# Where a chunk's key transposes and state products stand on TensorE, and a planner that counts a change of weight shape

## The chip, the cores and the metric

One core of a Trainium2 chip runs the whole kernel. The metric is the device time of one execution in microseconds (us), the median of the runs shown: 847.98 us of three runs (847.36 to 849.97). The profile is one further execution.

## The reference, cut to what matters

The kernel computes three stages in a row:

- A gated linear attention over 4 batches, 8 heads, 768 steps and head size 48: `state = f * state + k v^T`, `y = q state`, with `f` the sigmoid of `f_logit`.
- A two-layer network on the 3072 tokens (384 to 2048 to 384) with a leaky activation `max(h,0) + alpha*min(h,0)`.
- A routed layer of 8 experts (384 to 1024 to 384, ReLU). Tokens are dealt out by sorted gate logits with room for 384 tokens per expert; each token goes to one expert.

```python
for t in range(S):
    state = f[:, :, t, :, None] * state + np.einsum('bhd,bhe->bhde', k[:, :, t], v[:, :, t])
    y[:, :, t] = np.einsum('bhd,bhde->bhe', q[:, :, t], state)
...
g = np.maximum(h, 0.0) + alpha * np.minimum(h, 0.0)
...
out[mask] = np.maximum(x[mask] @ w1[e], 0.0) @ w2[e]
```

## The kernel before, in words

**The work.** Attention runs in 24 chunks of 128 steps (6 a batch, chunk i is number i % 6 of its batch). Three chunks make a block of 384 rows, eight blocks in all; a block's rows then go through the network (`ffn1`, line 1061) in products of 384 or 392 columns, here called FFN products. The attention of block b+1 is recorded with a lower number of priority than the FFN of block b (10b+10 against 10b+11), so on each engine it goes first wherever both could start. Beside blocks 0 and 1 the weights of the network are converted and split on VectorE and ScalarE (`narrow`, `split`); later the experts' weights are.

**A chunk** (`chunk`, line 1009) has these steps on TensorE; each fp32 product is two instructions in the trace, a transpose one:

- `s2` (line 900), on VectorE: the decayed keys `kT`, then the decayed queries `qT`.
- `s3` (909), the scores: 8 products, weights of 64 rows by 128 columns, into two PSUM banks; 16 instructions. Then two VectorE products with the causal mask write `A`, one for each bank; they are kept as `a["done"]`.
- `s3k` (924), the keys transposed: 4 transposes with weights of 128 by 128 into one bank, which ScalarE copies to `kt`. The last chunk of a batch has none.
- `s4` (935), the rows: weights of 128 by 64, 12 products with `A` and `v`, and 8 with the old state where the chunk isn't the first of its batch; 24 or 40 instructions of 128 columns. They are recorded `behind(a["done"])`.
- `s4s` (966), the state's products: 8 products of `kt` (128 by 64) and `v`, 16 instructions of 48 columns. Two VectorE operations on 64 partitions then make the new state, which the rows of the next chunk need. The last chunk of a batch has none.
- `s5` (988): ScalarE and VectorE turn the rows into the rounded input of the network.

The steps share three PSUM banks (`bank`, line 659, `bufs=3`): scores take two, transposes, rows and state's products one each.

**The order.** Nothing of this runs in the order in which it is written. `Plan.record` (206) keeps every operation with a price (`cost`, 544), and `Plan.schedule` (328) deals them out on a made-up clock: again and again it takes, over all engines, the operation that could start first; among those of one time the lowest priority number, then the one recorded first. VectorE may pass over one for another up to `PATIENCE` = 170 ns later. `behind(ops)` (182) makes a *soft* dependence: the operation is offered only once all of `ops` have been given a start. It is no semaphore; it only changes the order. The order so found is what every engine's queue then holds, and on the chip an instruction waits for its own inputs and for all that stands ahead of it in its queue.

Where the planner sees TensorE idle it puts filler products (`fill`, 448; line 1670 in the profile) of 512 columns into a free bank; nothing reads them. TensorE's price is the product's columns at 2.4 GHz (twice that at the slow clock), with nothing for what stood ahead of it:

```python
            price = op.cost[e]
            if e == "tensor":
                self.fill(free[e], t)
                slow = self.slow(t)
                if op.load:
                    mm[1] = max(mm) + op.load * slow
                    t = max(t, mm[1])
                price *= slow
```

An fp32 product with one side of 64 costs `2 * max(m, n) / 1.2 / 2 + 4`, so 110.7 ns for a score or a row product and 57.3 ns for one of the state's; a transpose costs 110 ns.

Of the kernel before, what the change touches and what calls it, by code (L numbers as in the profile page):

```python
# [28 lines left out]
HP = H // 2  # L29
# [48 lines left out]
SAME = {"vector": 125.0, "scalar": 150.0}  # L78
PATIENCE = 170.0
URGENT = 80.0  # L80
WINDOW, BUSY = 10240 / 3, 3060.0

LAGS = {"tensor": 200.0, "vector": 165.0, "scalar": 150.0, "gpsimd": 110.0, "sync": 120.0}
# [51 lines left out]
class Op:  # L135
    def __init__(self, idx, engines, calls, prio):
        self.idx, self.engines, self.calls, self.prio = idx, engines, calls, prio
        self.deps, self.soft, self.next, self.first, self.uses = set(), set(), [], [], []
        self.cost, self.load, self.columns, self.bytes, self.held = {}, 0.0, 0.0, 0, ()
        self.extra = 0.0  # L140

    def arenas(self):
        return {g.tag.arena for g in self.uses if g.tag.arena}
# [2 lines left out]
class Plan:  # L146
# [59 lines left out]
    def record(self, engines, method, a, k, slack=0.0):  # L206
        outs = accesses(a[:1]) + accesses(k.get(n) for n in ("out", "accum_out"))
        ins = accesses(a[1:]) + accesses(x for n, x in k.items() if n not in ("out", "accum_out"))
        if method == "matmul" and not (k["start"] and k["stop"]):

            outs = [self.ghosts[outs[0].tensor.name].ap]
        op = self.add(engines, lambda e, b: getattr(e, method)(*[b(x) for x in a], **{n: b(x) for n, x in k.items()}), outs, ins)  # L212
        op.slack = slack
        for e in engines:
            op.cost[e] = cost(e, method, outs, ins)
        if method in ("matmul", "transpose") and ins[0].dtype in (F32R, BF):
            op.load = free_size(ins[0]) / 1.2 if ins[0].dtype == F32R else 27.0
            op.held = {o for o, b in self.written.get(ins[0].tensor.name, []) if o is not op and meets(region(ins[0]), b)}
        if "tensor" in engines:
            n = free_size(ins[1]) if method == "matmul" else 256  # L220
            rows = ins[0].ap[0][1] / 128 * (0.5 if free_size(ins[0]) == 64 else 1.0)
            op.columns = n * rows * (4 if method == "matmul" and ins[0].dtype == F32 else 1)
        if "dma" in method:
            op.bytes = dma_bytes(outs + ins)
            op.extra = self.extra if "indirect" in method else 0.0
        return op
# [101 lines left out]
    def schedule(self):  # L328
# [10 lines left out]
        free["tensor"] = 800.0  # L339
        avail = {e: [] for e in self.ENGINES}  # L340
        mm, hw, dma = [0.0, 0.0], 600.0, [0.0, 0.0]

        def offer(op):
            since = max([g.since for g in op.uses if g.slot] + [d.start for d in op.soft], default=0.0)
# [21 lines left out]
        for _ in ops:  # L366
            best = None
            for e in self.ENGINES:
                wait, own, near = PATIENCE if e == "vector" else 0.0, None, []
                for op in avail[e]:  # L370
                    since = max(op.ready[e], free[e])
                    if best is not None and since > best[0] or own is not None and since > own[0] + wait:
                        continue
                    t = first(op, e)
                    if t is None or len(op.engines) > 1 and not self.better(op, e, t, free):
                        continue
                    key = (t, op.prio, op.idx, e, op)
                    if wait:
                        near.append(key)
                    if own is None or key < own:  # L380
                        own = key
                if near:

                    h = min((k for k in near if k[0] <= own[0] + wait), key=lambda k: k[1])
                    if URGENT <= h[1] < own[1] and own[0] + own[4].cost[e] > h[0] + 60.0:
                        fits = [k for k in near if k[0] + k[4].cost[e] <= h[0] + 60.0]
                        own = min(fits, default=h)
                if own is not None and (best is None or own < best):
                    best = own
            assert best, "no instruction can start"  # L390
            t, _, _, e, op = best
            for x in op.engines:
                avail[x].remove(op)
            for g in op.first:
                g.since, g.slot = self.place(g, ())
                g.slot.busy = True
                g.tag.given += 1
            price = op.cost[e]
            if e == "tensor":
                self.fill(free[e], t)  # L400
                slow = self.slow(t)
                if op.load:
                    mm[1] = max(mm) + op.load * slow
                    t = max(t, mm[1])
                price *= slow
                mm[0] = t
                self.count(t, t + price, op.columns)
            op.engine, op.start = e, t
            for a in op.arenas():
                a.left, a.turn = a.left - 1, max(a.turn, t + 1.0)  # L410
            free[e] = op.end = t + price
            if op.bytes:
                at = op.end
                if e == "sync":
                    hw = at = max(hw, at) + 450.0
                lane = e == "sync"
                dma[lane] = max(dma[lane], at + 650.0) + op.bytes / (300.0 if lane else 200.0)
                op.end = dma[lane] + 1000.0 + op.extra
            for g in op.uses:
                g.uses -= 1  # L420
                g.end = max(g.end, op.end)
                if not g.uses:
                    g.slot.busy, g.slot.free = False, g.end + 100.0
            for n in op.next:
                n.left -= 1
                if not n.left:
                    offer(n)
# [206 lines left out]
class Kernel:  # L634
# [265 lines left out]
    def s2(self, i):  # L900
        nc, a = self.nc, self.A[i]
        n = HP * SEG
        for name, dec in (("k", a["qr"][:, 1:n + 1].rearrange("p (g t) -> p g t", g=HP)[:, :, 1:]),
                          ("q", a["pf"].rearrange("p (g t) -> p g t", g=HP)[:, :, 1:])):
            t = a[name + "T"] = self.ap.tile([128, HP, C], F32, name=name + "T", bufs=2)
            self.claim(t)
            nc.vector.tensor_tensor(t, a[name], dec, OP.mult)

    def s3(self, i):

# [13 lines left out]
    def s3k(self, i):  # L924
# [3 lines left out]
        p = self.bank()  # L928
        t = a["kt"] = self.ap.tile([128, HP, 128], F32, name="kt", bufs=2)
        self.claim(t)  # L930
        for g in range(HP):
            nc.tensor.transpose(p[:, g * 128:(g + 1) * 128], a["kT"][:, g, :], self.ident)
        nc.scalar.activation(t.rearrange("p a b -> p (a b)"), p, AF.Copy)

    def s4(self, i):
# [30 lines left out]
    def s4s(self, i):  # L966
# [2 lines left out]
        if c == NCH - 1:  # L969
            return  # L970
        p = self.bank()
        for g in range(HP):
            for s in range(2):
                r = slice(s * 64, s * 64 + 64)
                nc.tensor.matmul(p[r, g * D:(g + 1) * D], a["kt"][:, g, r], a["v"][:, 2 * g + s, :D], start=True, stop=True)
        pv = p[:, :HP * D].rearrange("p (g e) -> p g e", g=HP)
        new = self.st[(i + 1) % 2]
# [874 lines left out]
```

## Time and profile before

| what | number |
|---|---|
| median of three runs | 847.98 us (847.36 to 849.97) |
| profiled execution | 851.19 us |
| its span, first to last instruction | 849.3 us |
| around the span | 1.89 us |
| TensorE busy | 820.0 us, 97% |
| VectorE busy | 564.8 us, 66% |
| ScalarE busy | 349.6 us, 41% |
| mean granted TensorE clock | 0.989 |

PE is TensorE's products, PEld its weight loads, DVE VectorE, ACT ScalarE, POOL GpSimd. A timeline row merges instructions of one kind that follow each other; its second number runs to the modelled end of the last, which reaches into the next row, so what a group takes of TensorE is read from its start to the start of the next row. Rows, state's products, and their joint runs all show as `bank<-early 128*64`: x40 is a chunk's rows, x16 of 48 columns its state's products, x56 the two together; `64*128` is the scores, and x32 that begins with them is scores and state's products together. FFN products carry `rounded` and `weights`.

### The profile page before, as it was taken

The numbers are of one execution on the slowest core, as the hardware profiler recorded it, in microseconds if no ns is written. First come the engines' busy times: TensorE is split into PE (matmuls) and PEld (weight loads), VectorE is DVE, ScalarE is ACT, GpSimd is POOL, SyncE is SP. The second block draws the span as 40 slices with busy tenths as digits, with TensorE's granted clock in tenths as the row PEclk, the third lists the DMA queues.
The fourth block names the chain that finished last, engine by engine and source line by source line (L and its number), as shares of the span: only waits on it lengthen the run. The fifth ranks groups of instructions, "written<-read, shape, count | busy, mean of one in ns | idle before, by whom it ended". The sixth has DMA issues, their size and how long they took to land. (4 is left out here: it accounts for less than half of the span.)

```text
span 849.3 us, 16038 instructions
## 1 busy us (share of the span) xinstructions
PE 820.0 (97%) x6122; PEld 756.5 (89%) x6122; DVE 564.8 (66%) x1308; ACT 349.6 (41%) x742; POOL 113.9 (13%) x105
## 2 busy tenths in 40 slices
PE   6999989999999999999999999999999999999995
PEld 3687889999999999999999999888788999899995
DVE  6899976977866966966975754655767658452220
ACT  3577665355555355555455443420122212222220
POOL 3111011210200200300300000000202302311211
PEclk7999999999999999999999999999999999999998
DMA  8895202599889688988878770003878775687400
GB/s 177 221 315 135 48 20 75 136 289 281 231 274 292 136 291 256 236 278 279 248 237 290 251 240 29 1 10 134 312 277 329 316 288 183 246 314 230 164 28 33
DMA packets 92792, 172.60 MB, mean 203 GB/s; under 512 B 31674, under 2 KB 61378, under 8 KB 92706
## 3 DMA queue, kind: packets, MB, share of 16 engines
q1 hardware_dynamic: 89490, 162.04, 60.0%
q0 software_dynamic: 3072, 9.44, 3.2%
q8 instruction: 50, 0.82, 0.4%
q14 instruction: 36, 0.29, 0.1%
q10 hardware_dynamic: 144, 0.01, 0.0%
HBM read 111.69 MB, written 59.77 MB: 202 GB/s over the span
## 5 line engine op out<-in xcount | busy, mean ns | idle before, releaser
L212 PE MATMUL bank<-rounded,weights 128*128 128x384 f32 (+1 forms) x1740 | 354.4, 344 | 1.2 <-POOL weights L212 0.5
L212 PE MATMUL bank<-weights,rounded 128*128 128x392 f32 (+1 forms) x1620 | 325.1, 344 | 3.0 <-ACT weights L212 2.3
L212 PEld LDWEIGHTS bank<-rounded,weights 128*128 128x128 f32 (+1 forms) x1740 | 302.4, 187 | 7.7 <-issue 2.3
L212 PEld LDWEIGHTS bank<-weights,rounded 128*128 128x128 f32 x1620 | 287.5, 189 | 5.6 <-issue 3.2
L212 ACT ACTIVATE rounded<-bank 128x384 fp32r<-128x384 f32 x110 | 54.1, 492 | 201.1 <-PE bank L212 188.4
L212 DVE TENSOR_TENSOR early<-early 128x384 fp32r<-128x384 f32 (+2 forms) x196 | 120.0, 629 | 16.1 <-ACT early L212 15.1
L212 PEld LDWEIGHTS bank<-early 128*64 128x64 f32 (+2 forms) x1696 | 98.3, 153 | 20.9 <-issue 10.4
L212 PE MATMUL bank<-early 128*64 128x128 f32 (+3 forms) x1696 | 110.2, 269 | 2.7 <-DVE early L212 1.5
L212 DVE SCALAR_TENSOR_TENSOR common<-common,rest,bank 128x384 f32<-128x384 f32 x128 | 77.9, 608 | 47.1 <-ACT common L232 46.1
L212 ACT ACTIVATE early<-early 128x384 fp32r<-128x384 f32 (+2 forms) x177 | 95.4, 548 | 31.9 <-DMA wd<-early 20.4
L212 POOL TENSOR_TENSOR rounded<-common,rounded 128x384 fp32r<-128x384 f32 x36 | 49.4, 1373 | 435.0 <-ACT rounded L212 398.0
L232 ACT ACTIVATE common<-bank 128x384 f32<-128x384 f32 x128 | 62.6, 489 | 71.4 <-PE bank L212 70.9
L212 ACT ACTIVATE rounded<-common 128x384 fp32r<-128x384 f32 x118 | 62.0, 525 | 65.9 <-DVE common L212 62.8
L212 DVE SCALAR_TENSOR_TENSOR rounded<-bank,rounded 128x384 fp32r<-128x384 f32 x62 | 34.5, 556 | 50.2 <-ACT rounded L212 48.3
L212 DVE TENSOR_TENSOR rounded<-common,rounded 128x384 fp32r<-128x384 f32 x82 | 46.5, 566 | 28.7 <-ACT rounded L212 20.3
L212 DVE TENSOR_TENSOR_SCAN early<-early 128x516 f32<-128x516 f32 x48 | 61.9, 1289 | 1.9 <-ACT early L212 1.6
L212 ACT ACTIVATE common<-bank 128x384 f32<-128x384 f32 x48 | 23.3, 492 | 71.4 <-PE bank L212 69.7
L212 POOL DMA_INDIRECT out_dram<-common,late x24 | 25.5, 1061 | 167.8 <-ACT common L212 115.7
L212 DVE TENSOR_TENSOR late<-late,cols 128x1536 bf16<-128x1536 bf16 (+3 forms) x53 | 42.7, 817 | 0.2
L212 POOL DMA_INDIRECT common<-x2d,late x24 | 25.9, 1077 | 90.2 <-DVE late L212 58.6
L212 DVE TENSOR_TENSOR rounded<-bank,rounded 128x384 fp32r<-128x384 f32 x48 | 26.3, 555 | 10.8 <-ACT rounded L212 10.3
L212 DVE TENSOR_TENSOR early<-bank,mask 128x512 f32<-128x512 f32 x48 | 31.0, 684 | 3.2 <-PE bank L212 2.9
(110 smaller groups left out, 488.7 us busy)
## 6 DMA issues: line engine op xcount, KB each, us to landing
wd<-early SPq DMA_DIRECT2D x128, 384.0 KB
weights<-wd SPq DMA_DIRECT2D x64, 768.0 KB
early<-in_w_dram SPq DMA_DIRECT2D x64, 384.0 KB
early<-in_fkq_dram SPq DMA_DIRECT2D x46, 288.0 KB
raw<-in_w_in_dram SPq DMA_DIRECT2D x16, 384.0 KB
raw<-in_w_out_dram SPq DMA_DIRECT2D x16, 384.0 KB
early<-in_v_dram SPq DMA_DIRECT2D x24, 192.0 KB
x2d<-common SPq DMA_DIRECT2D x24, 192.0 KB
```

The lines of the kernel that those rows point to most:

```text
L212: op = self.add(engines, lambda e, b: getattr(e, method)(*[b(x) for x in a], **{n: b(x) for n, x in k.items()}), outs, ins)
L232: return e.activation(b(out), b(x), AF.Relu, scale=-1.0)
```

## The change

The planner keeps the form of the last TensorE operation: how many rows its weights have, and whether they have 64 columns. Where an operation's form differs from the last one's, its start is put off by 92 ns; where the form is the same but the last was short (price up to 130 ns) and this one isn't, by 72 ns; and after either, the next operation by 80 ns. This is added to the made-up clock after the choice of the operation; fillers don't change the form. `s2` keeps its two products as `a["rows"]`; the transposes of `s3k` stand behind them; the products of `s4s` stand behind `a["done"]`, the masks of the chunk's scores, as the rows do.

```diff
+TURN, LONGER, AGAIN = 92.0, 72.0, 80.0
...
+            op.form = ins[0].ap[0][1], free_size(ins[0]) == 64
...
+        form, short, again = None, False, 0.0
...
                 slow = self.slow(t)
+                t, again = t + again, 0.0
+                turn = TURN if op.form != form else LONGER if short and price > 130.0 else 0.0
+                if turn:
+                    t, again = t + turn, AGAIN
+                form, short = op.form, price <= 130.0
                 if op.load:
...
             nc.vector.tensor_tensor(t, a[name], dec, OP.mult)
+        a["rows"] = self.last(2)
...
-        for g in range(HP):
-            nc.tensor.transpose(p[:, g * 128:(g + 1) * 128], a["kT"][:, g, :], self.ident)
+        with self.behind(a["rows"]):
+            for g in range(HP):
+                nc.tensor.transpose(p[:, g * 128:(g + 1) * 128], a["kT"][:, g, :], self.ident)
...
-        for g in range(HP):
-            for s in range(2):
-                r = slice(s * 64, s * 64 + 64)
+        for g, s in [(g, s) for g in range(HP) for s in range(2)]:
+            r = slice(s * 64, s * 64 + 64)
+            with self.behind(a["done"]):
                 nc.tensor.matmul(p[r, g * D:(g + 1) * D], a["kt"][:, g, r], a["v"][:, 2 * g + s, :D], start=True, stop=True)
```

## Rows read from the trace of the kernel before

**Rows 1.** The page: busy time of the engines, granted clock in 40 slices.

```profile
PE 820.0 (97%) x6122; PEld 756.5 (89%) x6122; DVE 564.8 (66%) x1308; ACT 349.6 (41%) x742; POOL 113.9 (13%) x105
...
PEclk7999999999999999999999999999999999999998
```

**Rows 2.** Windows, all instructions: PE, PEld, DVE, ACT, POOL busy; clock, DMA.

```profile
0.00:41.76 41.76, 33.76 (x273) 20.12 (x274) 31.69 (x71) 16.78 (x33) 10.08 (x19) 0.88 0.84 196
41.76:123.40 81.64, 75.38 (x576) 68.08 (x575) 77.47 (x151) 58.70 (x142) 13.04 (x11) 1.00 0.51 138
...
163.60:560.00 396.40, 395.20 (x2897) 378.08 (x2894) 280.81 (x525) 199.43 (x412) 34.39 (x23) 1.00 0.72 224
560.00:620.00 60.00, 57.12 (x459) 47.74 (x458) 36.80 (x143) 5.91 (x12) 6.46 (x6) 1.00 0.50 190
```

**Rows 3.** Windows, the fillers (line 1670) alone: PE busy, PEld busy, clock, DMA.

```profile
0.00:41.76 41.76, 17.28 (x52) 5.53 (x52) 0.88 0.84 196
41.76:123.40 81.64, 4.26 (x16) 1.57 (x16) 1.00 0.51 138
...
560.00:620.00 60.00, 7.43 (x29) 2.47 (x29) 1.00 0.50 190
```

**Rows 4.** PE's timeline, chunks 7 and 8: start us, us, instruction, count.

```profile
149.99 1.76 PE L212 MATMUL bank<-early 64*128 64x128 f32 x32
151.69 1.50 PE L212 MATMUL bank<-rounded,weights 128*128 128x384 f32 x7
...
156.13 0.88 PE L212 MATMUL bank<-weights,rounded 128*128 128x392 f32 x4
156.93 0.67 PE L212 MATMUL bank<-early 128*64 128x48 f32 x16
157.53 0.81 PE L212 MATMUL bank<-weights,rounded 128*128 128x392 f32 x3
158.27 1.16 PE L212 MATMUL bank<-early 64*128 64x128 f32 x16
159.36 0.62 PE L212 MATMUL bank<-weights,rounded 128*128 128x392 f32 x2
...
163.94 1.77 PE L212 MATMUL bank<-weights,rounded 128*128 128x392 f32 x9
165.55 1.75 PE L212 MATMUL bank<-rounded,weights 128*128 128x384 f32 x9
167.13 1.78 PE L212 MATMUL bank<-weights,rounded 128*128 128x392 f32 x9
```

**Rows 5.** PE's timeline, chunks 15 and 16.

```profile
333.81 2.85 PE L212 MATMUL bank<-early 128*64 128x128 f32 x56
336.59 0.66 PE L212 MATMUL bank<-ident,early 128*128 128x128 f32 x4
337.00 1.13 PE L212 MATMUL bank<-rounded,weights 128*128 128x384 f32 x5
...
340.30 2.40 PE L212 MATMUL bank<-early 128*64 128x128 f32 x40
342.63 0.44 PE L212 MATMUL bank<-rounded,weights 128*128 128x384 f32 x1
```

**Rows 6.** DVE's timeline: state and masks of chunks 0 to 2, masks of chunk 10.

```profile
16.47 0.72 DVE L212 COPY early<-bank 64x192 f32<-64x192 f32 x2 [1.46 <-PE bank L212]
...
26.57 0.72 DVE L212 TENSOR_TENSOR early<-bank,early 64x192 f32<-64x192 f32 x2 [0.73 <-PE bank L212]
...
36.16 0.71 DVE L212 TENSOR_TENSOR early<-bank,early 64x192 f32<-64x192 f32 x2
...
37.96 1.29 DVE L212 TENSOR_TENSOR early<-bank,mask 128x512 f32<-128x512 f32 x2
...
208.34 1.29 DVE L212 TENSOR_TENSOR early<-bank,mask 128x512 f32<-128x512 f32 x2 [0.22 <-PE bank L212]
```

**Rows 7.** PE's timeline, chunk 2: state's products, fillers, scores.

```profile
34.06 0.67 PE L212 MATMUL bank<-early 128*64 128x48 f32 x16 [0.47 <-ACT early L212]
34.66 1.04 PE L1670 MATMUL bank<-ones 128*128 128x512 bf16 x4
36.29 2.19 PE L212 MATMUL bank<-early 64*128 64x128 f32 x32 [0.59 <-DVE early L212]
```

More of the change, by code (lines that the diff above doesn't have):

```diff
@@ L139, in __init__ @@
         self.cost, self.load, self.columns, self.bytes, self.held = {}, 0.0, 0.0, 0, ()
-        self.extra = 0.0
+        self.extra, self.form = 0.0, None
     def arenas(self):
```

## The prediction, made blind

> **What bounds the kernel now.** I read the page first, to see that TensorE is busy 97% of the span and holds the full clock after the first slice [rows 1]: the end moves only with what TensorE does or with what makes it wait. Then the windows by stage, to see where that changes. From 163.60 to 560.00 TensorE is busy 395.20 of 396.40 us; there only TensorE's own time counts, and no other engine can hold it up by more than 1.2 us in all [rows 2]. From 41.76 to 123.40 VectorE is the bound: 77.47 of 81.64 us busy, while TensorE has 6.26 us idle [rows 2] and 4.26 us of fillers [rows 3]. In the first 41.76 us TensorE has work for about 16 us beside 17.28 us of fillers [rows 2, 3]. From 560 to 620, routing, 29 fillers stand for work that isn't there [rows 3]. Last the timeline of TensorE, to see what a group costs beyond its products [rows 4, 5], and that of VectorE at the start [rows 6].
>
> **State's products, later chunks.** The change removes and adds no instruction; it moves 16 of them per chunk (and what follows from the new clock). What they cost depends on the neighbours. An FFN product takes (167.13 - 163.94) / 18 = 0.177 us [rows 4]. Beside the rows, the x56 run takes 336.59 - 333.81 = 2.78 us against 342.63 - 340.30 = 2.33 us for x40 [rows 5]: the state's products add 0.45 us. Joined to the scores they add 151.69 - 149.99 = 1.70 against 159.36 - 158.27 = 1.09 us [rows 4], so 0.61: 0.16 more. Alone between FFN products, from 156.13 to 158.27 there are 2.14 us; seven FFN products take 1.24 and the state's 0.45, which leaves 0.45. Of that, about 0.10 is the change into the scores, which stays (two such changes around the state's products share the rest); so alone they cost about 0.35 us more than beside the rows.
> From chunk 6 on there are 15 sets. By the timeline two stand alone (chunks 6 and 8), four are joined to scores (7, 10, 16, 19) and nine stand beside or inside the rows already. With `behind(a["done"])` they are offered when the second mask starts, as the rows are, and later in the list than the rows. In chunks with an old state, 16 row instructions need no mask result; they go first, the state's products next, the other 24 after them: one run, one shape. Gain: 2 x 0.35 + 4 x 0.16 = **1.3 us**. Bounds: 0 if the old places come back, 1.3 if every set joins its rows.
> The wait that this adds is only one of order. Behind the state's products on TensorE stand rows and FFN products; who waits for them is VectorE's state update and then the next chunk's rows, more than a chunk's scores later. That is hidden in the later stage by 396 us of TensorE work.
>
> **Where the bank comes from.** Scores hold two of the three banks and the rows the third, so the state's products can only take the bank that the first mask frees. The two masks take 1.29 us [rows 6], so it is free about 0.65 us after they start; the 16 row instructions that can run meanwhile take (40 products' worth 2.33 us) x 16/40 = 0.93 us [rows 5]. So I charge nothing for the bank.
> The Trainium skill, Perfetto Trace Analysis, section Identifying the Most-Contended Engine and what follows on consistent bubbles, says that the same gap repeated on the engine that should be saturated can mean that PSUM has no room for the next tile. The trace of before shows no such gap in the later stage, and no run here shows one yet; by that page's rule the state's products would be held up in each chunk, and the sum would be that of the second rival below.
>
> **State's products, first chunks.** In chunks 0 and 1 they stand ahead of the scores, in chunk 2 ahead of four fillers and the scores [rows 7], and VectorE makes the new state ahead of the masks: 0.72, 0.72 and 0.71 us, with 1.46 and 0.73 us of waiting for TensorE in front of the first two [rows 6]. Moved behind the masks, scores can come first and rows earlier; the states of chunks 0 and 1 are still needed before the rows of 1 and 2, that of chunk 2 isn't. At most the two waits and one update go, 1.46 + 0.73 + 0.71 = 2.9 us; at least nothing, if VectorE's next operation is late as well. VectorE has other work ready in this stretch only in part, so I take a third, **1.0 us**. It reaches the end: VectorE bounds the stage up to 123.40 and TensorE from then on, so VectorE's earlier start is useful TensorE work instead of fillers. What is late next is VectorE's own scans and weight conversion.
>
> **Transposes.** Four take 337.00 - 336.59 = 0.41 us [rows 5] and have the FFN products' shape, so between FFN products they cause no change of shape, and next to a run of another shape they can at best share one. Offered only when `qT` starts, they lie a VectorE operation later, with their bank taken later too, so scores get their two banks first. ScalarE's copy of `kt` and then the state's products wait for them, and those now wait for the masks anyway. I take 0.3 us of gain; bounds -0.8 to +0.8, a tenth of 0.41 in each of 20 chunks.
>
> **The planner's clock.** It now charges 172 ns for a change where it charged nothing; the rows show 0.16 to 0.35 us for one or two changes [rows 4]. It doesn't choose by that charge, so nothing is regrouped for its sake; but planned gaps of TensorE shrink, so fewer fillers are placed, and VectorE's, ScalarE's, SyncE's and POOL's queues are dealt out anew. The change adds no DMA and moves none by itself; a new order of SyncE's queue is hidden where DMA engines are busy 0.72 or less [rows 2]. Fillers and idle in the VectorE-bound stage are 10.5 us; the trace of before doesn't show what a new order makes of them. I bound it by a third of it either way, 3.5 us, and take 0.5 us of gain, since fillers there (4.26 us) can only get fewer by this.
>
> **The sum.** 1.3 + 1.0 + 0.3 + 0.5 = 3.1 us off the profiled execution's 851.19 us (849.3 span and 1.89 around it): 848.1. That execution lies 3.2 us above the median shown; off the median, 847.98 - 3.1 = **844.9 us**. About 0.3%, 2.5 us, is what a measurement of this kernel can tell from no change, so the forecast is just beyond it.
>
> **The rivals.**
> *Hidden at the start.* VectorE is late anyway, the fillers stay, and only the later chunks' 1.3 us is had: 846.7, no measurable change. For it: VectorE is busy 77.47 of 81.64 us [rows 2], and a wait on TensorE that goes may show up as one on ScalarE. Against it: the two waits are on the way to the first block's rows [rows 6].
> *State's products cut off from their rows, slower.* Place: TensorE in the later chunks. If the bank or `kt` comes only after the rows have run, FFN products fill in and the state's products stand alone in all 15 chunks. The price: nine sets lose 0.35 and four lose 0.35 - 0.16, so 3.2 + 0.8 = 3.9 us; with the first chunks' gain lost too, 851.9. It decides where the bank comes later than 0.93 us after the masks start; at 0.65 us it doesn't, but in the first chunk of a batch no state products of the old state cover the masks. For it: three banks for four users.
> *The VectorE-bound stage reshuffled for the worse.* The third taken as a bound above goes the other way, less the 1.3: about 850.2, at the edge of slower. The same reshuffle in its favour gives 841 to 842.
> *It doesn't do what it says.* The transposes are ready with `kT` all the same and start before the scores, and nine of 15 sets are beside the rows already; then all that is left is a replan of about zero: 848.
>
> **How the numbers follow.** The forecast has 0.42, the start hidden 0.24, cut off 0.09, reshuffled for the worse 0.10 (half of it beyond 0.3%), reshuffled in favour 0.08, no effect 0.07. Faster by over 0.3%: 0.42 + 0.08 = 0.50. Slower: 0.09 + 0.05 = 0.14. Within: the rest, 0.36. The range takes in the forecast with its bounds (-3.5 for the reshuffle, -1.9 for the start beyond what is taken) down to 839.5, and reaches up to 851.0, which leaves out most of the cut-off case.
>
> **What would show it.** In the timeline after: x56 runs in every chunk with a state and no lone x16 of 48 columns; scores of chunk 0 ahead of the state's products, and VectorE's waits of 1.46 and 0.73 us shorter; fewer than 16 fillers between 41.76 and 123.40; the first FFN product before 41.76. Lone sets after the rows would show the second rival; more idle of TensorE before 123.40 the third. I am wrong if the later chunks are grouped as I say and the time doesn't move with the first stage's end.

## The result and the profile after

The changed kernel takes 859.80 us (median of 4 runs, 857.84 to 863.66) against 848.45 us (4 runs, 847.36 to 849.97) for the kernel before, a ratio of 1.0134 [1.0110, 1.0157]. That is slower by some 11 us, where 3.1 us of gain were forecast, and above the range. The profiled execution took 863.66 us with a span of 861.8, so it lies 3.9 us above its median, much as the one of before does.

The page of the changed kernel answers [rows 1]:

```profile
PE 824.4 (96%) x6107; PEld 760.9 (88%) x6107; DVE 566.7 (66%) x1312; ACT 352.6 (41%) x742; POOL 103.4 (12%) x101
...
PEclk7999999999999999999999999999999999999998
```

In these profiled executions TensorE is busy 4.4 us longer and idle 8.1 us longer (861.8 - 824.4 = 37.4 against 849.3 - 820.0 = 29.3). Nothing in the page says where. Cutting both traces at equal clock times would not say it either, since the work in a window differs; so I cut them at equal work: at the first FFN product in TensorE's timeline, and at the 301st, the 2051st and the 2501st. The windows of the kernel before, from the second on (span, then PE, PEld, DVE, ACT and POOL busy, clock, DMA share; the first is in [rows 2]):

```profile
41.76:137.02 95.26, 89.00 (x664) 81.24 (x663) 81.77 (x161) 64.98 (x159) 13.04 (x11) 1.00 0.45 122
137.02:533.35 396.33, 395.28 (x3025) 377.52 (x3024) 291.33 (x544) 197.46 (x410) 38.99 (x27) 1.00 0.76 232
533.35:663.48 130.13, 126.59 (x938) 110.66 (x935) 84.23 (x284) 29.05 (x58) 12.99 (x13) 0.99 0.49 191
663.48:849.33 185.85, 175.34 (x1233) 166.92 (x1232) 75.75 (x251) 41.30 (x84) 38.84 (x36) 0.99 0.53 194
```

The same five pieces of work in the changed kernel:

```profile
0.00:38.43 38.43, 29.75 (x257) 18.88 (x257) 29.65 (x70) 16.31 (x32) 7.73 (x18) 0.87 0.84 201
38.43:141.12 102.69, 94.51 (x666) 84.45 (x667) 83.21 (x162) 66.84 (x159) 18.58 (x14) 0.97 0.45 120
141.12:540.41 399.29, 397.53 (x3024) 379.43 (x3024) 293.54 (x547) 199.62 (x411) 25.28 (x21) 1.00 0.75 230
540.41:673.77 133.36, 127.81 (x933) 110.90 (x931) 84.62 (x283) 28.66 (x58) 13.83 (x13) 0.99 0.50 195
673.77:861.78 188.01, 174.84 (x1233) 167.20 (x1232) 75.68 (x251) 41.17 (x84) 37.97 (x36) 0.98 0.51 185
```

| stretch | before | after | difference |
|---|---|---|---|
| to the first FFN product | 41.76 | 38.43 | -3.3 |
| 300 products, VectorE-bound stage | 95.26 | 102.69 | +7.4 |
| 1750 products, TensorE-bound stage | 396.33 | 399.29 | +3.0 |
| 450 products, routing and first experts | 130.13 | 133.36 | +3.2 |
| to the end | 185.85 | 188.01 | +2.2 |

No stretch alone is the loss. The start is faster, as forecast and by more, and every stretch behind it is slower, also the one of which the prediction said that no other engine can hold TensorE up there. Part of the 7.4 us is the granted clock, 0.97 against 1.00; the stretch of 1750 products ran at 1.00 in both kernels.

### The profile page after: what moved, and what is told of

Same layout as the page of the kernel before. It is cut to its first block, busy times and chain, and to the rows that moved or that the text cites. A ratio compares the mean times of both kernels' runs of the same rounds, so it can differ in the third digit from the quotient of the medians.

```text
span 861.8 us, 15984 instructions
## 1 busy us (share of the span) xinstructions
PE 824.4 (96%) x6107; PEld 760.9 (88%) x6107; DVE 566.7 (66%) x1312; ACT 352.6 (41%) x742; POOL 103.4 (12%) x101
## 5 line engine op out<-in xcount | busy, mean ns | idle before, releaser
L214 PE MATMUL bank<-rounded,weights 128*128 128x384 f32 x1740 | 356.2, 345 | 0.6 <-POOL weights L214 0.6
L214 PEld LDWEIGHTS bank<-rounded,weights 128*128 128x128 f32 x1740 | 304.2, 188 | 7.5 <-issue 1.5
L214 PEld LDWEIGHTS bank<-early 128*64 128x64 f32 (+2 forms) x1696 | 102.1, 155 | 24.4 <-DVE early L214 11.8
L214 PE MATMUL bank<-early 128*64 128x128 f32 (+3 forms) x1696 | 113.0, 272 | 5.0 <-DVE early L214 4.2
L214 POOL TENSOR_TENSOR rounded<-common,rounded 128x384 fp32r<-128x384 f32 x29 | 36.2, 1248 | 441.8 <-ACT rounded L214 407.0
L214 DVE TENSOR_TENSOR rounded<-common,rounded 128x384 fp32r<-128x384 f32 x89 | 50.7, 569 | 34.6 <-ACT rounded L214 29.8
```

## What the runs tell apart

Two questions stood first: is it the new order (the waits of transposes and state's products) or the planner's new charge; and if the charge, is it its size, the stretch where it acts, or that any other deal of the queues costs as much. All diffs are against the changed kernel, and every kernel computes the whole. Ratios are to the kernel before on the same chip, whose medians were between 846.27 and 849.1 us.

| label | what is left of the change | us | ratio, 95% |
|---|---|---|---|
| after_again | all | 861.09 | 1.0140 [1.0097, 1.0183] |
| charge_only | charge, no waits | 862.61 | 1.0169 [1.0142, 1.0197] |
| order_only | waits, no charge | 851.96 | 1.0039 [1.0022, 1.0056] |
| state_only | wait of the state's products alone | 852.17 | 1.0045 [1.0023, 1.0067] |
| tiny_charge | charge of 2 ns, no waits | 849.12 | 1.0029 [1.0010, 1.0047] |
| half_charge | half the charge, no waits | 859.10 | 1.0118 [1.0084, 1.0153] |
| shape_charge | waits, charge for shape alone | 853.32 | 1.0064 [1.0042, 1.0087] |
| margin | all, and 300 ns more for results to TensorE | 871.88 | 1.0291 [1.0266, 1.0316] |
| charge_first | waits, charge up to 120 us | 848.43 | 1.0019 [0.9999, 1.0038] |
| charge_mid | waits, charge from 120 to 520 us | 855.43 | 1.0117 [1.0085, 1.0148] |
| charge_last | waits, charge from 520 us | 855.04 | 1.0106 [1.0076, 1.0136] |
| order_late | waits from chunk 6 on, no charge | 846.16 | 0.9996 [0.9977, 1.0015] |
| shape_mid | as charge_mid, for shape alone | 854.16 | 1.0070 [1.0047, 1.0092] |
| shape_last | as charge_last, for shape alone | 854.80 | 1.0069 [1.0045, 1.0093] |
| last_extra | charge_last, gathers allowed 2 us more | 854.16 | 1.0067 [1.0045, 1.0089] |
| mid_pool | charge_mid, 900 ns more for GpSimd's results | 855.98 | 1.0084 [1.0057, 1.0111] |
| late_first | charge up to 120 us, waits from chunk 6 | 851.07 | 1.0028 [1.0007, 1.0048] |
| late_shape_first | the same, for shape alone | 851.47 | 1.0038 [1.0019, 1.0057] |

### Order or charge

**after_again** is the changed kernel once more, with no edit.

> The changed kernel once more, for a second profile. If the half clock between 40 and 80 us of its first profile (0.91 granted) belongs to the order, it comes again and the time is 859 to 864 us; if it belongs to that one execution, the granted clock there is 1.00, the time 857 to 860, and the first 300 FFN products still end 2 to 4 us later than before.

The loss repeats (1.0140), and so do the stretches: the five cuts fall at 37.61, 140.16, 540.07, 672.27 and 859.79 us. So does the low clock, 0.97 granted again from the first to the 301st FFN product. The loss belongs to the kernel, not to one execution.

**charge_only** takes out the waits, **order_only** the charge.

```diff
-        with self.behind(a["rows"]):
+        with nullcontext():
...
-            with self.behind(a["done"]):
+            with nullcontext():
```

> The planner's charge for a change of shape, with transposes and state's products offered as before. Theory A (the charge deals all queues anew, and its clock leaves engines no margin): 856 to 862 us, most of the loss. Theory B (the two soft waits do it, states and transposes come too late in the VectorE-bound stage): 846 to 851 us.

```diff
-TURN, LONGER, AGAIN = 92.0, 72.0, 80.0
+TURN, LONGER, AGAIN = 0.0, 0.0, 0.0
```

> The two soft waits with all three charges at zero. Theory A: 844 to 849 us, with first FFN products about 3 us earlier than before. Theory B: 855 to 861 us, with chunk 4's rows waiting some 2 us for VectorE as in the changed kernel.

The charge alone costs all of it (1.0169, not clearly apart from the whole change), the waits alone 0.4%: order_only fell between its two forecasts, and the charge is the larger part by far. The part that by itself adds no wait and no instruction is the costly one.

**state_only** is order_only with the transposes' wait taken out as well.

```diff
-TURN, LONGER, AGAIN = 92.0, 72.0, 80.0
+TURN, LONGER, AGAIN = 0.0, 0.0, 0.0
...
-        with self.behind(a["rows"]):
+        with nullcontext():
```

> Only the state's products wait, charges at zero. Theory A: 844 to 849 us, and state's products of chunk 6 on beside their rows. Theory B: over 853 us if the states are what comes too late, within 2 us of before if it is the transposes.

1.0045 against 1.0039, again between the forecasts: of the waits' cost the state's products have all that can be seen, the transposes' wait does nothing measurable either way.

### A new deal, or this charge

**tiny_charge** (charge_only with 2 ns) and **half_charge** (with half) ask whether any other deal of the queues is worse.

```diff
-TURN, LONGER, AGAIN = 92.0, 72.0, 80.0
+TURN, LONGER, AGAIN = 2.0, 2.0, 2.0
```

> Control: the kernel before with a charge of 2 ns in all three places, no soft waits, so nearly the same made-up clock but ties fall otherwise. Theory M (the charge takes away a margin): within 2 us of before, 847 to 851. Theory R (any re-dealing of the queues costs this much, since before is one lucky order): 853 us or more.

```diff
-TURN, LONGER, AGAIN = 92.0, 72.0, 80.0
+TURN, LONGER, AGAIN = 46.0, 36.0, 40.0
```

> Half the charge (46, 36, 40 ns), no soft waits. Theory M: between before and the full charge, 852 to 858, with FFN products 1000 to 2050 taking 230 to 231 us (228.9 before, 231.7 with the full charge). Theory R: anywhere from 848 to 864, and no order between none, half and full.

A charge too small to mean anything deals the queues anew for 0.3%; half the charge costs 1.2%, the whole 1.7%. So a real charge costs clearly more than this one new deal by itself. That the loss grows from half to whole is not shown: the two intervals meet, and between the 301st and the 2051st FFN product half the charge takes 401.6 us, the whole 401.1 (charge_only). For the products 1001 to 2050 theory M had asked for 230 to 231 us; they took 232.3. Only routing is clearly longer with the whole (133.6 against 130.6 us).

**shape_charge** keeps the charge for a change of shape and drops the one for a long operation behind a short one of its shape.

```diff
-TURN, LONGER, AGAIN = 92.0, 72.0, 80.0
+TURN, LONGER, AGAIN = 92.0, 0.0, 80.0
```

> The changed kernel without the charge where the shape stays and only the length grows (72 ns at zero), which is mostly transposes before FFN products and the small products of the routing. Theory M in its narrow form (it is this part, charged though the trace shows about nothing for transposes, that makes the made-up clock too slow): 849 to 853. In its wide form (any charge that brings the made-up clock to the chip's): 856 to 861.

1.0064, at the upper end of what the narrow form asked for. In the nested series waits, shape, length the ratios are 1.0039, 1.0064, 1.0134: of some 11 us, 3.3 us come with the waits, 2 with the shape's charge and 6 with the length's. The parts don't add up in every order (the charge without the waits costs no less than with them), so these are shares along this path only. Between the 301st and the 2051st product the length's charge is also one that the chip doesn't ask for: from start to start in TensorE's timeline, a transpose and the FFN product behind it together take 0.29 us, as a transpose (0.109) and an FFN product (0.178) do elsewhere, against 72 + 80 ns charged on top. In routing it is not so: behind a product of 8 columns an FFN product takes 0.26 us, some 0.08 more than elsewhere.

### Which stretch

The charge is confined to one part of the planner's made-up clock; the waits stay.

```diff
                 turn = TURN if op.form != form else LONGER if short and price > 130.0 else 0.0
+                turn = turn if t < 120000.0 else 0.0
```

> The changed kernel with the charge counted only up to 120 us of the made-up clock (the stage in which VectorE is the bound). Theory S (the charge costs in each stage apart: fewer fillers and a dropped clock at the start, no margin in the FFN stretch, a worse routing): first 300 FFN products end at about 141 us as in the changed kernel, FFN products 1000 to 2050 take 229 us, time 851 to 855. Theory F (what goes wrong at the start shifts all that follows): 857 to 861, nearly the whole loss.

```diff
+                turn = turn if 120000.0 <= t < 520000.0 else 0.0
```

> The changed kernel with the charge counted only from 120 to 520 us (FFN beside attention). Theory S: start and routing as with the orders alone, FFN products 1000 to 2050 take 231 to 232 us, time 853 to 856. Theory F: within 2 us of the orders alone, 849 to 853.

```diff
+                turn = turn if t >= 520000.0 else 0.0
```

> The changed kernel with the charge counted only from 520 us (routing and experts). Its queues are those of the orders alone up to there. Theory S: 852 to 856, with the routing stretch (FFN products 2150 to 2300) 2 to 4 us longer than before. Theory F: 849 to 853, that stretch within 1 us of before.

In the first 120 us it costs nothing beyond the waits (1.0019, and 848.43 us is below both forecasts); in the later two it costs 0.7 to 0.8% more than the waits alone, each by itself, about 6 us, as theory S asked. The windows show that each stays where the charge is. First order_only, TensorE-bound stage and routing, with no charge in either:

```profile
140.43:535.91 395.48, 394.88 (x3025) 378.54 (x3025) 292.13 (x544) 196.97 (x410) 33.93 (x27) 1.00 0.76 232
535.91:664.47 128.56, 124.96 (x936) 109.06 (x933) 84.33 (x284) 29.00 (x58) 12.99 (x13) 1.00 0.50 193
```

Then charge_mid, with 5.6 us more in the first and nothing in the second:

```profile
140.66:541.78 401.12, 397.26 (x3026) 379.58 (x3025) 290.24 (x545) 198.57 (x411) 33.06 (x26) 1.00 0.75 229
541.78:670.30 128.52, 125.83 (x934) 108.97 (x932) 84.49 (x283) 28.63 (x58) 13.38 (x13) 1.00 0.51 193
```

And charge_last, the other way round, with 5.2 us more in the second:

```profile
138.27:533.72 395.45, 394.85 (x3025) 378.51 (x3025) 292.64 (x544) 197.75 (x410) 33.89 (x27) 1.00 0.76 233
533.72:667.49 133.77, 127.97 (x937) 111.38 (x934) 84.36 (x284) 28.95 (x58) 13.24 (x13) 0.99 0.50 194
```

What TensorE waits for is new in each. Its waits in charge_mid from 140.66 to 541.79 (total us, times, longest):

```profile
PE bank L214 <- POOL rounded L214: 1.4, 2, 0.7
PE bank L214 <- PE bank L214: 0.6, 1, 0.6
PE bank L214 <- ACT rounded L214: 0.6, 1, 0.6
PE bank L214 <- ACT early L214: 0.5, 1, 0.5
PE bank L214 <- DVE common L214: 0.3, 1, 0.3
```

The same view of order_only, 140.43 to 535.9, has two waits, of 0.3 and 0.2 us. In routing, charge_last from 534 to 667:

```profile
PE bank L214 <- DMA common<-x2d,late: 4.2, 7, 1.5
PE bank L214 <- DMA weights<-wd: 1.4, 1, 1.4
```

and order_only from 536 to 664:

```profile
PE bank L214 <- DVE late L214: 1.8, 3, 0.9
PE bank L214 <- DMA common<-x2d,late: 1.5, 3, 0.7
```

The waits on transfers grow from 1.5 to 5.6 us: the gathered rows and an expert's weights are late for a TensorE that comes to them by the new order. These listed waits explain 3.4 - 0.5 = 2.9 of charge_mid's 5.6 us and 5.6 - 3.3 = 2.3 of charge_last's 5.2. The rest is time that the view counts as busy: in charge_mid TensorE is busy 397.26 against 394.88 us for the same products, so in stalls too short to be listed; in charge_last also in a dip of the clock, 0.96 granted from 600 to 640 us, behind the longest of the waits on gathered rows. Counted in the timeline start to start over the products 1001 to 2050, the changed kernel takes 3.0 us more than before over the same work: 0.8 at the changes from an FFN product to a row (0.147 us beyond the product on average against 0.090), 1.0 between FFN products, 0.6 between scores, and 0.7 at one listed wait ahead of routing.

**order_late** lets the first six chunks go as before, without the charge.

```diff
-TURN, LONGER, AGAIN = 92.0, 72.0, 80.0
+TURN, LONGER, AGAIN = 0.0, 0.0, 0.0
...
-        with self.behind(a["rows"]):
+        with self.behind(a["rows"]) if i >= 6 else nullcontext():
...
-            with self.behind(a["done"]):
+            with self.behind(a["done"]) if i >= 6 else nullcontext():
```

> The two soft waits only from chunk 6 on, no charge: the part of the change that the forecast valued at 1.3 us. Queues are those of before up to about 120 us. If the state's products beside their rows are worth that, FFN products 300 to 1000 take 166.5 us against 167.4 before, and the time is 0 to 2 us under before; the soft waits in the first six chunks would then be what makes the orders alone slower (by 2.9 us there).

0.9996, no difference; its 301st FFN product stands at 136.91, as before (137.02), where order_only has 140.43. So the 0.4% of the waits is lost in the first six chunks, and grouping in the later ones gains what there is to gain: from the 301st to the 2051st FFN product it takes 532.27 - 136.91 = 395.36 us, against 396.33 before, 1.0 less. The other executions with the waits and no charge in this stretch agree (395.2 to 395.5 us in order_only, state_only, charge_last and last_extra), and tiny_charge, without the waits, takes 396.4.

### Is it lost margin

The theory that was left: the old planner held TensorE for faster than it is, so its real TensorE came late to each result, and that lateness was room for the others; with a truer clock it comes in time by plan and too early in fact. **margin** gives room back, flat: 300 ns more for every result that goes to TensorE.

```diff
-    return LAGS[d.engine] + (40.0 if e == "gpsimd" else 0.0)
+    return LAGS[d.engine] + (40.0 if e == "gpsimd" else 300.0 if e == "tensor" else 0.0)
```

> The changed kernel whole, and the planner counts 300 ns more from any other engine's result to a TensorE instruction. Theory M: the waits of TensorE on VectorE in FFN products 1000 to 2050 go, that stretch takes 229 to 230 us, and the time is 850 to 856. Theory R or the orders alone: no better than the changed kernel, 858 us or more.

Split: products 1001 to 2050 take 229.57 us, as the theory asked (before 228.90, changed 231.92); but products 301 to 1000 take 170.35 (167.43 and 167.38), where TensorE now waits 3.3 us on VectorE between 140 and 165 us, and the part behind the 2501st product 194.0 (185.9 and 188.0). The whole kernel is 3% slower than before, where 850 to 856 us had been forecast. In this form room is no remedy: the wait moves to other places.

**shape_mid** and **shape_last** drop the length's charge in one stretch at a time.

```diff
-TURN, LONGER, AGAIN = 92.0, 72.0, 80.0
+TURN, LONGER, AGAIN = 92.0, 0.0, 80.0
...
+                turn = turn if 120000.0 <= t < 520000.0 else 0.0
```

> Charge from 120 to 520 us of the made-up clock as in charge_mid, but with the 72 ns for a longer product of the same shape at zero (in this stretch that is transposes before FFN products, where the trace shows no such time). Theory O (the charge harms where it charges what the chip doesn't take): within 2 us of the orders alone, 848 to 852, FFN products 300 to 1000 in 166 to 167 us. Theory W (a made-up clock that matches the chip leaves no margin for the other engines): 852 to 857, that stretch 169 us or more.

```diff
-TURN, LONGER, AGAIN = 92.0, 72.0, 80.0
+TURN, LONGER, AGAIN = 92.0, 0.0, 80.0
...
+                turn = turn if t >= 520000.0 else 0.0
```

> Charge from 520 us on as in charge_last, with the 72 ns at zero (there it falls on small products of the routing before FFN products, where the trace does show about 83 ns). Theory O: no different from charge_last, 852 to 856, since that charge is real. Theory W: 848 to 853 if a slower made-up clock there is what puts TensorE ahead of the transfers; no wait on the experts' weights at about 610 us.

1.0070 and 1.0069, against 1.0117 and 1.0106 with it: rather more than half of what each stretch loses beyond the waits goes with the length's charge, the rest stays with the shape's. They don't decide between the theories. In shape_mid products 301 to 1000 take 167.94 us, between what O and W asked. In shape_last the time is in O's range, but the ratio lies below charge_last's, which O did not ask for; the wait on the experts' weights, which W wanted gone, fell from 1.4 to 0.8 us. By the same cuts, the TensorE-bound stage takes 397.73 us (order_only 395.48, charge_mid 401.12), routing 131.22 (128.56, 133.77). The intervals, some 0.2% wide on either side, don't allow a finer split.

**last_extra** asks for gathered rows earlier, **mid_pool** counts GpSimd as later, each against the largest listed wait of its stretch.

```diff
+                turn = turn if t >= 520000.0 else 0.0
...
-        self.plan.extra = 3500.0
+        self.plan.extra = 5500.0
```

> charge_last with 5500 ns instead of 3500 counted for an indirect transfer's landing. If TensorE's waits on the experts' weights and gathered rows (about 6 us between 590 and 655 in charge_last) are what the charge costs there, and more margin gives them back, 848 to 852; if the longer landing only moves the products elsewhere, 853 or more.

```diff
+                turn = turn if 120000.0 <= t < 520000.0 else 0.0
...
-    return LAGS[d.engine] + (40.0 if e == "gpsimd" else 0.0)
+    return LAGS[d.engine] + (40.0 if e == "gpsimd" else 900.0 if d.engine == "gpsimd" and e == "tensor" else 0.0)
```

> charge_mid with 900 ns more counted from a GpSimd result to TensorE. If GpSimd's late low parts (two waits of 0.7 us, and the products behind them) are the main cost of the charge in the FFN stretch, the waits go and the time is 850 to 853; if the cost is spread over waits on VectorE and ScalarE too, 853 to 856.

The waits go in both, the time only in part. In last_extra the gathers' waits fall from 4.2 to 1.0 us and routing from 133.77 to 129.91, 3.9 of the 5.2 us back, and with them goes charge_last's dip of the clock (0.96 from 600 to 640 us, here 1.00). The weights' 1.4 us stay, and the whole kernel is still 0.7% slower than before, where the orders alone are 0.4% and charge_last 1.1%; the intervals of last_extra and charge_last overlap. Its 854.16 us is in the range forecast for a longer landing that only moves the products elsewhere. So late gathers, with the dip that follows the longest of them, are part of the price there; that they are most of it is what one profile says and the times don't show. In mid_pool the waits on GpSimd fall from 1.4 to 0.3 us and the products 301 to 1000 from 170.16 to 167.91, but those from 1001 to 2050 rise from 230.97 to 232.59: 0.6 of 5.6 us back. There the listed wait is a symptom of the order as a whole.

**late_first** and **late_shape_first** look for a version better than both kernels: the charge only up to 120 us, the waits only from chunk 6 on.

```diff
+                turn = turn if t < 120000.0 else 0.0
...
-        with self.behind(a["rows"]):
+        with self.behind(a["rows"]) if i >= 6 else nullcontext():
...
-            with self.behind(a["done"]):
+            with self.behind(a["done"]) if i >= 6 else nullcontext():
```

> What was free or better in the other runs, together: the soft waits from chunk 6 on, the charge up to 120 us of the made-up clock. If stages add up, FFN products 300 to 1000 take 165.5 to 166.5 us and the time is 843 to 847, level with before or up to 0.4% under. If the first stage's order is chance, its first 300 FFN products end 0 to 4 us later than before's and the time is 847 to 851.

```diff
-TURN, LONGER, AGAIN = 92.0, 72.0, 80.0
+TURN, LONGER, AGAIN = 92.0, 0.0, 80.0
...
+                turn = turn if t < 120000.0 else 0.0
...
-        with self.behind(a["rows"]):
+        with self.behind(a["rows"]) if i >= 6 else nullcontext():
...
-            with self.behind(a["done"]):
+            with self.behind(a["done"]) if i >= 6 else nullcontext():
```

> The same with the 72 ns at zero. If the charge for length is harmful in the first stage too, 1 to 3 us under the run beside it; if the first stage's order is chance, either sign.

1.0028 and 1.0038: no. In late_first the products 301 to 1000 take 166.2 us, as stages that add up would have it, but its 301st product comes 2.8 us later than before's. Nothing that was tried beats the kernel before; the nearest, order_late, is the same.

## Why the prediction was wrong, by its steps

**State's products, later chunks: right.** The runs are there; TensorE's timeline after, in two later chunks, answers [rows 4, 5]:

```profile
205.18 1.16 PE L214 MATMUL bank<-early 64*128 64x128 f32 x16
206.28 0.66 PE L214 MATMUL bank<-ident,early 128*128 128x128 f32 x4
206.69 0.42 PE L214 MATMUL bank<-rounded,weights 128*128 128x384 f32 x1
207.12 2.86 PE L214 MATMUL bank<-early 128*64 128x128 f32 x56
209.91 0.66 PE L214 MATMUL bank<-ident,early 128*128 128x128 f32 x4
...
415.92 0.67 PE L214 MATMUL bank<-early 128*64 128x48 f32 x16
```

The x56 run is rows and state's products in one shape; the lone set at 415.92 is the only one left from 140 us on. Within the run the products mostly stand behind all 40 row instructions (here from 209.35 us), not between the 16 and the 24 as forecast, which costs no further change of shape. Alone, the grouping is worth the 1.0 us that order_late shows between the 301st and the 2051st product (1.3 forecast).

**Where the bank comes from: the charge of nothing right, its reason not tested.** The state's products stand in the run and don't wait ahead of it. But the bank had 209.35 - 207.12 = 2.23 us of rows to come free in, not the 0.93 of the forecast, since all 40 row instructions mostly go first. The x56 run of 2.86 us takes no longer than the 2.85 us of [rows 5], and there is no gap that repeats. So the trace doesn't show the sign that the Trainium skill's Perfetto Trace Analysis (Optimization Strategy, on consistent bubbles) gives for a lack of PSUM.

**First chunks: the mechanism right, its end wrong.** Scores of chunk 0 now stand ahead of the state's products, in TensorE's timeline after:

```profile
16.40 1.65 PE L214 MATMUL bank<-early 64*128 64x128 f32 x12
...
18.40 0.80 PE L214 MATMUL bank<-early 64*128 64x128 f32 x4
...
19.67 1.54 PE L214 MATMUL bank<-early 128*64 128x48 f32 x18
```

and VectorE, its timeline after, makes mask ahead of state, with waits of 0.54 and 0.30 us and none at the update of chunk 1, where [rows 6] had 1.46 and 0.73; but a copy ahead of the masks now waits 1.09 us, where it waited 0.29:

```profile
18.51 0.18 DVE L214 COPY early<-bank 128x24 f32<-128x24 f32 x1 [1.09 <-PE bank L214]
19.23 1.29 DVE L214 TENSOR_TENSOR early<-bank,mask 128x512 f32<-128x512 f32 x2 [0.54 <-PE bank L214]
20.82 0.72 DVE L214 COPY early<-bank 64x192 f32<-64x192 f32 x2 [0.30 <-PE bank L214]
...
29.22 0.32 DVE L214 TENSOR_TENSOR early<-bank,early 64x192 f32<-64x192 f32 x1
```

So VectorE's waits on TensorE up to the first FFN product fell from 2.5 us only to 1.9. The first FFN product came 3.3 us earlier, 1.0 was forecast; but 2.0 us of that are VectorE's work put off (29.65 us busy up to there, against 31.69 in [rows 2]), which is no gain where VectorE bounds. What failed is the sentence that this "reaches the end": 7.4 us are lost over the next 300 products. Up to the 301st product VectorE does about the same work in both (113.5 us before, 112.9 after) and is idle 28.3 us against 23.6. The fillers, forecast to get fewer than 16 behind the first FFN product, are 16 again; ahead of it they fell from 52 to 38 (windows after, line 1682 alone, to be read as in [rows 3]):

```profile
0.00:38.43 38.43, 13.30 (x38) 4.31 (x38) 0.87 0.84 201
38.43:123.40 84.97, 4.91 (x16) 1.59 (x16) 0.96 0.51 133
```

Six executions have one and the same order of TensorE in this stage, with the waits and no charge (order_only, charge_mid, charge_last, shape_mid, shape_last, last_extra). They reach the 301st product between 136.9 and 140.7 us, the three with the full clock from the first FFN product on at 136.9 to 138.3. From the first to the 301st product these three take 101.5 to 101.9 us and the others up to 103.3, against 95.26 before and 95.2 in order_late, both at the full clock. Two of them, order_only and then charge_last:

```profile
37.95:140.43 102.48, 93.86 (x675) 82.92 (x675) 82.99 (x155) 65.12 (x159) 21.21 (x17) 0.98 0.45 118
36.74:138.27 101.53, 92.34 (x676) 81.93 (x675) 82.97 (x155) 65.06 (x159) 21.28 (x17) 1.00 0.44 118
```

So this order loses its gain again even at the full clock, and the prediction counted the waits as a gain only. It does not follow from the waits alone in every deal: mid_pool, which has them too and counts GpSimd's results as later, reaches the 301st product at 135.2 us, earlier than any other run. The charge without the waits does no better there: 137.8 to 139.8 us in charge_only, half_charge, late_first and late_shape_first.

**Transposes: within the bounds.** order_only and state_only differ by less than their intervals.

**The planner's clock: the step that failed.** It took 0.5 us of gain, bounded it by 3.5 us either way, put all of it into the VectorE-bound stage, and said that the planner "doesn't choose by that charge, so nothing is regrouped". The charge moves the clock by which it deals all later work of every queue. Taken alone it costs 1.7% (14 us), and the two stretches where it costs were those that the prediction had covered: "no other engine can hold it up by more than 1.2 us in all", and "a new order of SyncE's queue is hidden where DMA engines are busy 0.72 or less". The second cover looked at the wrong queue, as views of the kernel after show, TensorE's waits from 540 to 672 and its timeline:

```profile
PE bank L214 <- DMA common<-x2d,late: 2.5, 5, 0.8
PE bank L214 <- DMA weights<-wd: 1.7, 1, 1.7
PE bank L214 <- DVE late L214: 1.2, 1, 1.2
```

```profile
614.30 1.83 PE L214 MATMUL bank<-weights,rounded 128*128 128x384 f32 x9 [1.69 <-DMA weights<-wd]
```

Before, the only wait on a transfer in this stretch (533 to 663) was one on gathered rows:

```profile
PE bank L212 <- DMA common<-x2d,late: 1.9, 1, 1.9
```

SyncE's queue there has the same order in both kernels (`x2d`, three weights, `x2d` twice, `mark`, weights). Its timelines, before and after, have the weights issued 66.2 and 65.9 us behind the 2051st FFN product:

```profile
599.50 13.32 SPq L1442 DMA_DIRECT2D weights<-wd  x13
...
606.35 12.13 SPq L1454 DMA_DIRECT2D weights<-wd  x12
```

What changed is TensorE's queue: between the gathered rows' transposes and the product that waits it has 29 FFN products, where before 36 stood, so it asks for the weights some 1.2 us earlier. The first cover mistakes what a busy TensorE means: that it is busy 395.20 of 396.40 us [rows 2] says that each result was there in time in that order, not that it would be in another.

**The rivals.** "Reshuffled for the worse" had the right sign and a fifth of the size (2.2 of some 11 us), and its place, the VectorE-bound stage, is one of several. "Cut off from their rows", the other slower one, did not happen. Nor did "it doesn't do what it says", since the sets moved; "hidden at the start" would have left no measurable change.

**What stays open.** That the charge is the cause, and in which stretches it costs, is shown; why a plan made with it runs slower is not. That the old, too fast clock served as margin fits the stretch of margin's run that came back (229.57 us), but a flat margin made the whole slower and half the charge cost as much as the whole in the TensorE-bound stage, so it is argued, not shown. Open are also which of the short stalls belongs to which engine, and why one deal of the first 140 us takes some 6 us longer behind the first FFN product than another.

## What to carry to other kernels

A schedule's cost model that is wrong about the bounding engine can still serve the kernel better than one that counts more of what the engine does, here by 1.3%, perhaps because its error is room for everyone who feeds that engine; a correction of it is a new schedule, to be tested by part and by stretch (a window on the made-up clock does that in three runs). A bounding engine that is busy 99% covers the order that it has, not the next one. And a wait that such a change shows need not be its price: taking one out gave back 3.9 of 5.2 us in one stretch (a dip of the clock included) and 0.6 of 5.6 in the other. Last, one profile is one execution: the same order reached the same product up to 3.8 us apart, so a difference of a few us between two profiles wants a second execution or the times of many.

## What was not expected of the hardware

The clock falls in the first 140 us in some of these executions, of one order not in each. In the changed kernel it falls to a granted 0.66 from 45 to 50 us in both of its profiled executions, behind 1.23 us of idle (1.12 in the second) and five fillers. Nine FFN products behind that take 48.94 - 46.16 = 2.78 us, 0.31 each, instead of 0.177 [rows 4]: most of them ran at the lower of the clock's two levels, 1.2 against 2.4 GHz. What it is worth shows in order_only and charge_last, whose TensorE has the same order up to 520 us. One window, first order_only:

```profile
75.00:85.00 10.00, 9.07 (x49) 7.68 (x49) 8.56 (x19) 8.06 (x21) 1.09 (x1) 0.83 0.11 28
```

then charge_last:

```profile
75.00:85.00 10.00, 9.03 (x57) 8.13 (x57) 9.72 (x21) 9.04 (x24) 2.34 (x2) 1.00 0.23 48
```

Between the 501st and the 601st operation of TensorE, about this window, order_only takes 95.35 - 76.60 = 18.75 us and charge_last 93.17 - 75.37 = 17.80. So 0.17 of 10 us less clock, 1.7 us, cost about 0.95. The changed kernel was granted 0.95 from 35 to 100 us, 3.3 us by the same sum: as an estimate, of the 7.4 us lost in this stage at most that, and rather half of it, is the clock. Charge_first, which has the changed kernel's TensorE order there and was granted 0.92 against 0.97 from the first to the 301st FFN product, took 1.8 us longer.

The end of the program varies too. From the start of GpSimd's last output transfer to the end of the span it took 849.33 - 842.18 = 7.1 us before, and 861.78 - 852.13 = 9.7 us after (9.3 when run again, 9.7 in charge_only and 9.6 in mid_pool, but 7.1 to 7.5 in every other run, half_charge among them). The 2.5 us more cover the whole +2.2 us of the last stretch, but this is no steady cost of the charge: it is absent in half_charge and there in mid_pool, which has no charge from 520 us on. The part ahead of it varies as well: from the 2501st FFN product to TensorE's last one, executions of one and the same order took 174.2 (charge_mid) to 177.3 us (before). No run was made for the cause of either, which stays open.
